# A two-branch attention kernel: PSUM banks, SBUF overlays and load queues of its first stage rearranged

## The chip, the cores and the metric

The kernel runs on one core of a Trainium2 chip. The metric is the time of one execution on the device, in microseconds (us). A core has five engines with a program each: TensorE (PE), VectorE (DVE), ScalarE (ACT), GpSimd (POOL) and SyncE (SP). They run side by side and wait for one another with semaphores; each executes its own instructions in the order in which they stand in its program. Sixteen DMA engines move data between HBM and SBUF; in this kernel the SyncE and ScalarE queues issue to them.

## The reference

Two attention branches read the same input `x` (2048 tokens x 512), and a gate mixes them per token.

```python
g = sigmoid((x * gate_w).sum(-1))
a = A(x)                       # recurrent memory, 64 segments of 32 tokens, one after the other
b = B(x)                       # 4 quarters of 512 tokens
out = g * a + (1 - g) * b

# A, segment s; mem is 8 tokens, first mem0
h = concat(mem, x[s])          # 40 tokens
q, k, v = h@Wq, h@Wk, h@Wv     # 32 heads of 128
o = softmax(mask(q k^T)) v @ Wo
mem, out_a[s] = o[:8], o[8:]

# B, quarter s; 32 heads of 16; M and z are sums over earlier quarters
p = softmax(q k^T + causal) v
mem_part = phi(q) M / (phi(q) z)
o = sig(beta) * mem_part + (1 - sig(beta)) * p
M += phi(k)^T v ;  z += sum phi(k)      # phi(t) = t + 1 for t > 0, else exp(t)
b = o @ wo
```

The kernel writes phi(t) as min(exp(t), 1) + max(t, 0).

## The kernel before

**Program and queues.** The Python code walks through the work once and appends instructions to a list for each engine (`Prog.op`, `Prog.dma`). Dependencies come from named resources: a reader waits for the last writer, a writer for the last writer and all readers. An instruction that waits stops everything behind it on its engine. GpSimd instructions also depend, each, on the GpSimd instruction ahead of them. A DMA frees what it reads only when it has landed.

**Stage one** (`b_projections`) has 64 pieces, numbered `n`. For each quarter of 512 tokens `pk` projects the keys (`wkB`) and the queries (`wqB`) of branch B in four slices of 128 features; the results are copied out of PSUM to staging tiles `stgk` (by VectorE) and `stgq` (by ScalarE), four of each, and stored to DRAM scratch. `pv` projects the values, copied into `V17`, on VectorE and ScalarE in turn, and stored. `kn` transposes a staged key slice, and `phi` makes its features in `phK`. From quarter 1 on `phi` also makes the query features, through a temporary `etmp` (five of them) into `stgp` (three), which are stored. `mz` adds phi(k)^T v to the memory sums in two long-held PSUM banks, from which `MZ16` is masked and stored. `x_chunk` transposes the next 512 tokens of x into `xT`. `gate_parts` computes the gate at pieces 36 and on.

`phi` has three instructions: the exponential on ScalarE at once, and, put off by one piece, a min with 1 (L622) and a max-and-add (L623), both on VectorE.

GpSimd makes constants. `plan_const` sets the first ones; `late_const`, called at piece 9, makes the mask `mneg` of branch A's loop, by memsets and 64 small selects (L414).

**The loads.** x, the three weights of B and small inputs are issued first, on SyncE. x is held in the space of `Wo_sb` until it is transposed. The loop's weights are in a list, `weights`: Wk, Wq and Wv in four loads of 1 MB each, Wo in four, and B's output weights `woB_sb` in eight small ones. Every fourth piece from piece 6 on takes one entry, the rest follow at the end. The big ones are issued on ScalarE's queue, in program order with its other work. First loads of branch B's attention (`bat.load`) come at pieces 50 to 56.

**The loop** (`plan_a`) starts with `left_units(0)`, projections for the memory rows of the first group, and then runs the 64 segments. Each is a hand-written order of units for TensorE (projections L947, mask and scores L1165 to L1172, the output projection L1000), and branch B's attention is woven into it. The loop's tiles (`in_a`) lie over those of stage one (`in_p`) in SBUF. `v.under` lists for each loop tile the stage-one tiles beneath it, and its first writer waits for their last uses: `QT_sb`, for instance, lies over `stgp`, so it waits until the stores from `stgp` have landed. GpSimd copies the x columns of a segment into `hT` (L1124) and the left queries into `QT_sb` (L1334).

**Banks.** `Banks.take` picks one of eight PSUM banks. It holds banks 0 and 1 back for long use, and while few whole pairs are free it prefers a bank whose neighbour is in use, as the loop needs pairs for its wide scores.

Of the kernel before, what the change touches and what calls it, by code (L numbers as in the profile page):

```python
# [5 lines left out]
ALU = mybir.AluOpType  # L6
AX = mybir.AxisListType
BF16 = mybir.dt.bfloat16
F32 = mybir.dt.float32
# [30 lines left out]
class Banks:  # L40
# [3 lines left out]
    def __init__(self, res):  # L44
        self.free = list(range(len(res)))
        self.res = res

    def take(self, long=False):
        assert self.free, "out of banks"
        f = self.free  # L50
        if long:
            c = [b for b in f if b < 2] or f
        else:
            whole = [b for b in f if b > 1 and b ^ 1 in f]
            c = [b for b in f if b not in whole and b > 1] if len(whole) <= 4 else [b for b in f if b > 1]
            c = c or [b for b in f if b > 1] or f
        b = c[0]
        f.remove(b)
        return b
# [165 lines left out]
def build(nc, es, A_x, A_mem0, A_Wq, A_Wk, A_Wv, A_Wo, B_wq, B_wk, B_wv, B_wo, B_beta, gate_w, out, dbg=None):  # L225
    v = NS()
    _, S, DM = A_x.shape
# [29 lines left out]
    def alloc(stack, *specs):  # L257
        at, spans = 0, {}
        for name, shape, dt, n in specs:
# [20 lines left out]
          ("aTg", [128, C, 128], BF16, 0), ("fold", [128, SEG], BF16, 0),  # L280
          ("WH", [128, DM], BF16, 0), ("WL", [128, DM], BF16, 0))
    esP = ExitStack()
    in_p = alloc(esP, ("wkB", [128, C, DM], BF16, 0), ("wqB", [128, C, DM], BF16, 0), ("phK", [128, 4, DM], BF16, 0), ("MZ16", [128, 544], BF16, 0),
          ("bmask", [128, 136], BF16, 0), ("mem0_sb", [128, DM], BF16, 0), ("gwr_sb", [128, 128], BF16, 0), ("beta_sb", [128, HB], BF16, 0),
          ("gB_sb", [128, HB], F32, 0), ("omgB_sb", [128, HB], F32, 0),
          ("etmp", [128, 512], BF16, 5), ("stgp", [128, 512], BF16, 3), ("stgk", [128, 512], BF16, 4), ("stgq", [128, 512], BF16, 4),
          ("V17", [128, 4, HB, 17], BF16, 0), ("wvB", [128, C, DM], BF16, 0))
    esP.close()
    v.stg = {"k": v.stgk, "q": v.stgq, "p": v.stgp}
    v.x_sb = v.Wo_sb[:, 0:NTT, :]  # L290
    esA = ExitStack()
    in_a = alloc(esA, ("xL", [128, C, SEG], BF16, 0), ("LN_sb", [128, 2, 512], BF16, 0), ("KTL", [128, H // 2, SEG, 2], BF16, 2), ("QTL", [128, H // 2, SEG, 2], BF16, 2),
          ("VL", [128, 2, 512], BF16, 2), ("KN_sb", [128, 2, 512], BF16, 0), ("QN_sb", [128, 2, 512], BF16, 0),
          ("KT_sb", [128, H // 2, SEG, 2], BF16, 0), ("QT_sb", [128, H // 2, L, 2], BF16, 0), ("V_sb", [128, 2, 512], BF16, 0),
          ("P_sb", [128, 2, 224], BF16, 0), ("R_sb", [128, 2, 160], F32, 0),
          ("OT_sb", [128, H, L], BF16, 0), ("OTL", [128, H, SEG], BF16, 2),
          ("oTt", [128, 16, 32], F32, 0), ("t1_sb", [128, DM], F32, 0), ("aT_st", [128, C, 128], BF16, 2))
    esA.close()
    v.under = {a: [p for p, (p0, p1) in in_p.items() if p0 < a1 + 64 and a0 < p1 + 64] for a, (a0, a1) in in_a.items()}

# [63 lines left out]
    weights = plan_loads(v, A_x, A_mem0, A_Wq, A_Wk, A_Wv, B_wq, B_wk, B_wv, B_wo, B_beta, gate_w)  # L364
    pieces = b_projections(v)
    bat = v.bat = BAttn(v)
    gates = gate_parts(v)
    x_chunk(v, 0)
    for n in range(len(pieces)):
        if n in (8, 20, 32):  # L370
            x_chunk(v, (n + 4) // 12)
        if n == 9:
            sigmoid(v, v.beta_sb[:, :], v.gB_sb, v.omgB_sb, "gB", [Rs("beta")])
            for src, dst, res in ((v.gB_sb, v.gBp, "gB"), (v.omgB_sb, v.omgBp, "omgB")):
                for j in range(4):
                    q = slice(32 * j, 32 * j + 32)
                    P.op("gp", lambda g, src=src, dst=dst, q=q, j=j: g.tensor_copy(dst[q, :], src[q, :].rearrange("p (f j) -> p f j", j=4)[:, :, j]),
                         reads=[Rs(res)], writes=[Rs(res + "p")], name="%sp%d" % (res, j))
            v.late_const()
        if n >= 36 and n % 2 == 0 and gates:  # L380
            gates.pop(0)()
        pieces[n]()
        if n in (50, 52, 54, 56):
            bat.load(0, n // 2 % 2, "kv"[n // 54])
        if weights and n % 4 == 2 and n > 5:
            weights.pop(0)()
    while weights:
        weights.pop(0)()


    v.home = late_home
    plan_a(v, NSEG_RUN)
    for go in v.g_out:
        if go.count:
# [72 lines left out]
def plan_loads(v, A_x, A_mem0, A_Wq, A_Wk, A_Wv, B_wq, B_wk, B_wv, B_wo, B_beta, gate_w):  # L467
    P, Rs, C, M = v.P, v.Rs, v.C, v.M
    xsrc = A_x[0].rearrange("(i p) d -> p i d", p=128)

    def ld(grp, dst, src, res, name):
        P.dma(P.group(grp), lambda s: s.dma_start(dst, src), writes=[Rs(res)], name=name)

    def x(k):
        for h in range(2):
            o = 4 * k + 2 * h
            ld("x%d%d" % (k, h), v.x_sb[:, o:o + 2, :], xsrc[:, o:o + 2, :], "x_sb%d%d" % (k, h), "dma_x%d%d" % (k, h))
    x(0)
    for nm, dst, src in (("wk", v.wkB, B_wk), ("wq", v.wqB, B_wq), ("wv", v.wvB, B_wv)):
        ld("b" + nm, dst[:, :, :], src.rearrange("(c p) n -> p c n", p=128), nm + "B", "dma_" + nm)  # L480
    x(1)
    g = P.group("small")
    for fn, res in ((lambda s: s.dma_start(v.beta_sb[:, :], B_beta.rearrange("(o n) -> o n", o=1).to_broadcast([128, v.HB])), "beta"),
                    (lambda s: s.dma_start(v.gwr_sb[0:C, :], gate_w.rearrange("(c p) -> c p", p=128)), "gwr"),
                    (lambda s: s.dma_start(v.mem0_sb[0:M, :], A_mem0[0]), "mem0")):
        P.dma(g, fn, writes=[Rs(res)], name="dma_" + res)
    x(2)
    x(3)

    def weight(grp, dst, src, res, c):  # L490
        P.dma(grp, lambda s: s.dma_start(dst[:, c, :], src[c * 128:(c + 1) * 128].rearrange("p h e -> p (h e)")),
              writes=[Rs(res)], name="dma_%s%d" % (res, c), eng="act")
    pend = []
    for res, dst, src in (("Wk", v.Wk_sb, A_Wk), ("Wq", v.Wq_sb, A_Wq), ("Wv", v.Wv_sb, A_Wv)):
        grp = P.group(res)
        for c in range(C):
            pend.append(lambda grp=grp, dst=dst, src=src, res=res, c=c: weight(grp, dst, src, res, c))
    grp = P.group("Wo")
    wosrc = v.A_Wo.rearrange("h e d -> e h d")
    for q in range(4):  # L500
        def wo(q=q):
            P.dma(grp, lambda s: s.dma_start(v.Wo_sb[:, 8 * q:8 * q + 8, :], wosrc[:, 8 * q:8 * q + 8, :]), 
                  writes=[Rs("Wo")] + ([Rs("x_sb%d%d" % (k, h)) for k in (2 * q, 2 * q + 1) for h in range(2)] if q < 2 else []), name="dma_Wo%d" % q, eng="act")
        pend.append(wo)

    def wob():
        grp = P.group("bwo")
        rows = B_wo.rearrange("(f g j d) n -> g j d f n", f=C, g=2, j=4)
        for j in range(4):
            for g in range(2):  # L510
                o = 32 * j + 16 * g
                P.dma(grp, lambda s, j=j, g=g, o=o: s.dma_start(v.woB_sb[o:o + 16, :, :], rows[g, j]), writes=[Rs("woB")], name="dma_woB%d%d" % (j, g))
    pend.append(wob)
    return pend


# [80 lines left out]
def b_projections(v):  # L597
# [14 lines left out]
    def phi(src, rsrc, dst, wres, name, eng, then):  # L612

        n = st["n"] = st["n"] + 1
        et = v.etmp[n % 5][:, :]
        re = Rs("etmp%d" % (n % 5))
        P.op("act", lambda a: a.activation(et, src, ACT.Exp), reads=[rsrc], writes=[re], name=name + "_e")
        if len(dst.shape) == 3:
            src, et = (t.rearrange("p (a d) -> p a d", d=128) for t in (src, et))

        def rest():
            P.op(eng, lambda d: d.tensor_scalar(et, et, 1.0, None, op0=ALU.min), reads=[re], writes=[re], name=name + "_m")  # L622
            P.op(eng, lambda d: d.scalar_tensor_tensor(dst, src, 0.0, et, ALU.max, ALU.add), reads=[rsrc, re], writes=wres, name=name)  # L623
            then()
        later.append(rest)
# [25 lines left out]
    def pv(sb, tt):  # L651
# [7 lines left out]
            return ins  # L659
        P.op("pe", fp, reads=x_res(v, sb) + [Rs("wvB")], writes=[v.rbank[bk]], name="pvn%d_%d" % (sb, tt))  # L660
        rv = Rs("V17_%d" % tt)
        v.evac("act" if tt % 2 else "dve", v.V17[:, tt, :, 0:16], v.pb[bk].rearrange("p (h d) -> p h d", d=16), [bk], [rv], "evv%d_%d" % (sb, tt))
        store("stv%d" % sb, v.vd[sb, :, tt, :], v.V17[:, tt, :, :].rearrange("p h w -> p (h w)"), [rv, Rs("V17o")], [Rs("vd%d_%d" % (sb, tt))],
              "stv%d_%d" % (sb, tt))
        BK.give(bk)
# [248 lines left out]
def plan_a(v, nseg):  # L914
# [208 lines left out]
    def x_copy(s):  # L1123
        P.op("gp", lambda gq: gq.tensor_copy(hT[s % 2][:, :, M:SEG], xT[:, :, SEG * s:SEG * (s + 1) - M]),  # L1124
             reads=x_all, writes=[Rs("hTx%d" % (s % 2))], name="hx%d" % s)

    def segment(s, fill):
# [207 lines left out]
             reads=[Rs("QTL%d_%d" % (par, b)) for b in range(2)], writes=[Rs("QTl")], name="qtl%d" % s)  # L1335
        if s + 1 < nseg:
            x_copy(s + 1)
        for u in ORDER[r]:
            units[u]()

# [88 lines left out]
```

The softmax here doesn't subtract the row's maximum and nothing guards it: scores larger than these inputs give would overflow.

## Time and profile before

| | before |
|---|---|
| time, median of 3 runs | 948.48 us (947.42 to 949.68) |
| span of the profiled run | 946.2 us |
| PE busy | 875.4 us, 93% of the span |
| DVE busy | 635.1 us, 67% |
| ACT busy | 575.4 us, 61% |
| POOL busy | 243.6 us, 26% |
| DMA moved | 51.36 MB, most of it in the first 88 us |
| stage one, first to last projection | from 7.3 to 70.8 us |
| the loop's first segment, to the start of the second | 77.03 to 99.86 us |
| the second segment, to the start of the third | 99.86 to 113.24 us |

Busy time is counted over the whole execution; a stretch of the timeline is needed to see what one stage waits for. In the timeline a row has the start, the length of a run of like instructions, engine, line, output and inputs, the count, and in square brackets the idle time ahead of it with the instruction that ended it. In the bracket a wait that has several causes is put down to the last one.

### The profile page before, as it was taken

How to read it: one execution, taken by the hardware profiler on the slowest of the kernel's cores; microseconds unless marked ns; L12 is line 12 of the kernel's file. 1: busy time of each engine (PE TensorE's matmuls, PEld its weight loads, DVE VectorE, ACT ScalarE, POOL GpSimd, SP SyncE). 2: the span in 40 equal slices, each digit the busy share in tenths (PEclk: the TensorE clock that was granted, in tenths of full speed). 3: DMA queues.
4: the chain of work that ended last, by engine and by line, in shares of the span. 5: the costliest groups of instructions: out<-in, count | busy, mean ns of one | idle time of the engine just before them, and what ended most of it. 6: DMA issues, size and time to landing. Idle time of an engine off the chain costs nothing. (4 is left out here: it accounts for less than half of the span.)

```text
span 946.2 us, 51712 instructions
## 1 busy us (share of the span) xinstructions
PE 875.4 (93%) x23175; PEld 466.7 (49%) x23182; DVE 635.1 (67%) x1388; ACT 575.4 (61%) x1339; POOL 243.6 (26%) x553
## 2 busy tenths in 40 slices
PE   8886989999899999999999989999999999999885
PEld 3443545555454545555455545545455555544442
DVE  4763666676666786776776777667767677677564
ACT  3542666666666766666666665666666666664553
POOL 3610222222222231322222232222222232221110
PEclk9997999999999999999999999999999999999999
DMA  9997000000001121101001110100101110000110
GB/s 305 371 343 247 13 13 16 15 21 18 22 9 38 32 54 28 27 16 27 16 21 49 32 44 20 28 15 19 41 16 41 31 43 24 24 3 9 37 37 8
DMA packets 66052, 51.36 MB, mean 54 GB/s; under 512 B 34464, under 2 KB 64296, under 8 KB 64296
## 3 DMA queue, kind: packets, MB, share of 16 engines
q1 hardware_dynamic: 59944, 31.29, 12.1%
q10 hardware_dynamic: 5888, 16.78, 5.0%
q8 instruction: 182, 2.98, 1.3%
q14 instruction: 38, 0.31, 0.1%
HBM read 33.47 MB, written 14.57 MB: 51 GB/s over the span
## 5 line engine op out<-in xcount | busy, mean ns | idle before, releaser
L801 ACT ACTIVATE PT<-ps 128x1024 bf16<-128x1024 f32 x160 | 163.8, 1024 | 1.8
L947 PE MATMUL ps<-Wv_sb,hT 128*32 128x512 bf16 x2048 | 143.5, 385 | 0.0
L947 PE MATMUL ps<-Wq_sb,hT 128*32 128x512 bf16 x2048 | 134.5, 380 | 0.0
L947 PE MATMUL ps<-Wk_sb,hT 128*32 128x512 bf16 x2048 | 132.7, 379 | 0.0
L808 POOL TENSOR_SCALAR_AFFINE_SELECT PT<-PT 128x512 bf16<-128x512 bf16 (+1 forms) x96 | 75.8, 789 | 199.9 <-ACT PT L801 175.3
L1000 PE MATMUL ps<-Wo_sb,OT_sb 128*32 128x512 bf16 x2048 | 123.4, 380 | 0.3 <-DVE OT_sb L357 0.2
L357 DVE CAST V_sb<-ps 128x512 bf16<-128x512 f32 x128 | 88.5, 691 | 47.7 <-PE ps L947 47.7
L1218 POOL TENSOR_TENSOR P_sb<-P_sb,R_sb 128x64 bf16<-128x64 bf16 x128 | 47.4, 371 | 280.0 <-PE ps L1172 166.7
L959 DVE STREAM_TRANSPOSE QT_sb<-QN_sb 128x256 f32<-128x256 f32 x128 | 56.7, 443 | 77.9 <-ACT QN_sb L355 70.1
L355 ACT ACTIVATE QN_sb<-ps 128x512 bf16<-128x512 f32 x128 | 77.1, 602 | 31.3 <-PE ps L947 28.8
L355 ACT ACTIVATE OT_sb<-ps 128x320 bf16<-128x320 f32 x128 | 56.0, 437 | 61.9 <-PE ps L1241 59.7
L1011 DVE TENSOR_TENSOR WL<-ps,WH 128x256 bf16<-128x256 f32 x128 | 54.3, 424 | 46.0 <-ACT WH L355 42.5
L1181 ACT ACTIVATE P_sb<-ps 128x224 bf16<-128x224 f32 x128 | 45.2, 353 | 60.8 <-PE ps L1172 60.8
L947 PEld LDWEIGHTS ps<-Wk_sb,hT 128*32 128x32 bf16 x2048 | 54.0, 97 | 48.7 <-ACT KN_sb L355 1.2
L357 DVE CAST OT_sb<-ps 128x320 bf16<-128x320 f32 x128 | 61.8, 483 | 20.3 <-PE ps L1241 18.9
L947 PEld LDWEIGHTS ps<-Wq_sb,hT 128*32 128x32 bf16 x2048 | 49.7, 96 | 44.6 <-ACT hT L355 9.3
L959 DVE STREAM_TRANSPOSE KT_sb<-KN_sb 128x256 f32<-128x256 f32 x128 | 56.5, 441 | 21.3 <-ACT KN_sb L355 19.1
L1000 PEld LDWEIGHTS ps<-Wo_sb,OT_sb 128*32 128x32 bf16 x2048 | 48.1, 96 | 45.1 <-DVE OT_sb L357 5.5
L787 PE MATMUL ps<-QTj,KTj 32*128 32x256 bf16 (+1 forms) x768 | 62.9, 255 | 4.3 <-ACT PT L801 3.6
L355 ACT ACTIVATE WH<-ps 128x256 bf16<-128x256 f32 x64 | 24.6, 384 | 62.6 <-PE ps L1000 59.7
L1205 ACT ACTIVATE R_sb<-ps 128x160 f32<-128x160 f32 x128 | 39.1, 305 | 35.8 <-PE ps L1198 35.8
L1228 PE MATMUL ps<-P_sb,V_sb 32*128 32x40 bf16 x2048 | 36.3, 178 | 22.2 <-ACT OT_sb L355 7.7
(131 smaller groups left out, 1578.5 us busy)
## 6 DMA issues: line engine op xcount, KB each, us to landing
Wk_sb<-in_A_Wk_dram ACTq DMA_DIRECT2D x4, 1024.0 KB, 6.9
Wq_sb<-in_A_Wq_dram ACTq DMA_DIRECT2D x4, 1024.0 KB, 8.2
Wv_sb<-in_A_Wv_dram ACTq DMA_DIRECT2D x4, 1024.0 KB, 7.8
Wo_sb<-in_A_Wo_dram ACTq DMA_DIRECT2D x4, 1024.0 KB, 10.9
scr_vd<-V SPq DMA_DIRECT2D x16, 136.0 KB, 6.3
Vj<-scr_vd SPq DMA_DIRECT2D x32, 68.0 KB, 2.5
Wo_sb<-in_A_x_dram SPq DMA_DIRECT2D x8, 256.0 KB, 6.1
scr_kTd<-stgk SPq DMA_DIRECT2D x16, 128.0 KB, 8.0
```

Source lines behind the costliest of these rows:

```text
L355: P.op("act", lambda a: a.activation(dst, src, ACT.Copy), reads=[v.rbank[k] for k in bks], writes=dres, name=name)
L357: P.op("dve", lambda d: d.tensor_copy(dst, src), reads=[v.rbank[k] for k in bks], writes=dres, name=name)
L787: ins = pe.matmul(v.pb[bks[x]][:, 256 * e + o:256 * e + o + w], KT[e][r, 128 * kc:128 * (kc + 1)], QT[r, q0:q0 + w], start=True, stop=True ...
L801: P.op("act", lambda a: a.activation(pt[:, :, :], v.ps[:, bks[0]:bks[1] + 1, :], ACT.Exp, scale=v.SCALE_B), reads=[v.rbank[b] for b in bks ...
L808: P.op("gp", lambda g: g.affine_select(mv, mv, [[0, mv.shape[1]], [1, 128]], ALU.is_ge, 0.0, base=0, channel_multiplier=-1), reads=[rp], w ...
L947: ins = pe.matmul(pb[bk][SEG * j:SEG * (j + 1), :], lhs(c), cols(w, j) if split else w[:, 512 * j:512 * (j + 1)], start=(c == 0), stop=(c ...
L959: P.op("dve", lambda d: d.transpose(to, src), reads=reads, writes=writes, name=name)
L1000: ins = pe.matmul(pb[bk][SEG * j:SEG * (j + 1), :], lhs(4 * k + j), Wo_sb[:, 4 * k + j, :], start=(first and k == ks[0]), stop=False, skip ...
L1011: P.op("dve", lambda d: d.tensor_tensor(lo[:, c], pb[bk][:, c], hi[:, c], ALU.subtract), reads=[rbank[bk], Rs(res[0][hf])], writes=[Rs(res ...
L1181: P.op("act", lambda a: a.activation(P_sb[:, b, :], pb[bk][:, 0:224], ACT.Exp, scale=SCALE), reads=[rbank[bk]], writes=[Rs("P%d" % b), Rs( ...
L1205: P.op("act", lambda a: a.activation(R_sb[:, b, :], pb[bk][:, 224:384], ACT.Ln), reads=[rbank[bk]], writes=[Rs("R%d" % b)], name="ln%d_%d" ...
L1218: P.op(ENG["n"], lambda d: d.tensor_tensor(left(P_sb), left(P_sb), grp04(R_sb[:, b, :]), ALU.mult), reads=[Rs("R%d" % b)], writes=[Rs("P%d ...
```

## The change

Its purpose is to let stage one and the loads beside it run with fewer waits, and to let the loop start without waiting for stores. It has these parts:

- In stage one `Banks.take` gives the bank that came free longest ago (`oldest`); at the start of the loop the old rule returns and the free list is sorted.
- The order of the stage-one tiles and of the loop's tiles is changed, so that the tiles that the first segment writes lie over inputs and temporaries rather than over tiles that are read by stores. `KTL`, `QTL` and `VL`, two of each, are split, and their second ones put last.
- The loads of Wk, Wq and Wv start at piece 2 instead of 6. Wo is taken out of the list and issued on SyncE after all of stage one; `woB_sb` is loaded in segment 1 of the loop.
- The first loads of branch B's attention come at pieces 36 to 42 instead of 50 to 56.
- The min of the query features (L622 before) moves from VectorE to GpSimd; that of the key features stays on VectorE.
- All copies of the values to `V17` are on ScalarE.

```diff
+        self.oldest = True
...
+        elif self.oldest:
+            c = [b for b in f if b > 1] or f
...
-    in_p = alloc(esP, ("wkB", [128, C, DM], BF16, 0), ("wqB", [128, C, DM], BF16, 0), ("phK", [128, 4, DM], BF16, 0), ("MZ16", [128, 544], BF16, 0),
+    in_p = alloc(esP, ("wkB", [128, C, DM], BF16, 0), ("wqB", [128, C, DM], BF16, 0), ("phK", [128, 4, DM], BF16, 0), ("etmp", [128, 512], BF16, 5),
...
-          ("etmp", [128, 512], BF16, 5), ("stgp", [128, 512], BF16, 3), ("stgk", [128, 512], BF16, 4), ("stgq", [128, 512], BF16, 4),
-          ("V17", [128, 4, HB, 17], BF16, 0), ("wvB", [128, C, DM], BF16, 0))
+          ("gB_sb", [128, HB], F32, 0), ("omgB_sb", [128, HB], F32, 0), ("wvB", [128, C, DM], BF16, 0), ("MZ16", [128, 544], BF16, 0),
+          ("stgk", [128, 512], BF16, 4), ("stgq", [128, 512], BF16, 4), ("V17", [128, 4, HB, 17], BF16, 0), ("stgp", [128, 512], BF16, 3))
...
+          ("OT_sb", [128, H, L], BF16, 0), ("OTL", [128, H, SEG], BF16, 2), ("KTL1", LT, BF16, 0), ("QTL1", LT, BF16, 0), ("VL1", [128, 2, 512], BF16, 0),
...
-        if n in (50, 52, 54, 56):
-            bat.load(0, n // 2 % 2, "kv"[n // 54])
-        if weights and n % 4 == 2 and n > 5:
+        if n in (36, 38, 40, 42):
+            bat.load(0, n // 2 % 2, "kv"[n // 40])
+        if weights and n % 4 == 2:
             weights.pop(0)()
-    while weights:
-        weights.pop(0)()
+    v.wo_load()
...
+    v.BK.oldest = False
+    v.BK.free = sorted(v.BK.free)
     plan_a(v, NSEG_RUN)
...
-            P.op(eng, lambda d: d.tensor_scalar(et, et, 1.0, None, op0=ALU.min), reads=[re], writes=[re], name=name + "_m")
+            P.op("gp" if name[3] == "q" else "dve", lambda d: d.tensor_scalar(et, et, 1.0, None, op0=ALU.min), reads=[re], writes=[re], name=name + "_m")
...
-        v.evac("act" if tt % 2 else "dve", v.V17[:, tt, :, 0:16], v.pb[bk].rearrange("p (h d) -> p h d", d=16), [bk], [rv], "evv%d_%d" % (sb, tt))
+        v.evac("act", v.V17[:, tt, :, 0:16], v.pb[bk].rearrange("p (h d) -> p h d", d=16), [bk], [rv], "evv%d_%d" % (sb, tt))
...
+        if s == 1:
+            v.wob_load()
```

More of the change, by code (lines that the diff above doesn't have):

```diff
@@ L282, in build @@
     esP = ExitStack()
-    in_p = alloc(esP, ("wkB", [128, C, DM], BF16, 0), ("wqB", [128, C, DM], BF16, 0), ("phK", [128, 4, DM], BF16, 0), ("MZ16", [128, 544], BF16, 0),
+    in_p = alloc(esP, ("wkB", [128, C, DM], BF16, 0), ("wqB", [128, C, DM], BF16, 0), ("phK", [128, 4, DM], BF16, 0), ("etmp", [128, 512], BF16, 5),
           ("bmask", [128, 136], BF16, 0), ("mem0_sb", [128, DM], BF16, 0), ("gwr_sb", [128, 128], BF16, 0), ("beta_sb", [128, HB], BF16, 0),
-          ("gB_sb", [128, HB], F32, 0), ("omgB_sb", [128, HB], F32, 0),
-          ("etmp", [128, 512], BF16, 5), ("stgp", [128, 512], BF16, 3), ("stgk", [128, 512], BF16, 4), ("stgq", [128, 512], BF16, 4),
-          ("V17", [128, 4, HB, 17], BF16, 0), ("wvB", [128, C, DM], BF16, 0))
+          ("gB_sb", [128, HB], F32, 0), ("omgB_sb", [128, HB], F32, 0), ("wvB", [128, C, DM], BF16, 0), ("MZ16", [128, 544], BF16, 0),
+          ("stgk", [128, 512], BF16, 4), ("stgq", [128, 512], BF16, 4), ("V17", [128, 4, HB, 17], BF16, 0), ("stgp", [128, 512], BF16, 3))
     esP.close()
@@ L291, in build @@
     esA = ExitStack()
[L292 to L296, printed above, removed]
+    LT = [128, H // 2, SEG, 2]
+    in_a = alloc(esA, ("xL", [128, C, SEG], BF16, 0), ("LN_sb", [128, 2, 512], BF16, 0), ("KTL0", LT, BF16, 0), ("QTL0", LT, BF16, 0), ("VL0", [128, 2, 512], BF16, 0),
+          ("KN_sb", [128, 2, 512], BF16, 0), ("QN_sb", [128, 2, 512], BF16, 0), ("KT_sb", LT, BF16, 0), ("QT_sb", [128, H // 2, L, 2], BF16, 0),
+          ("V_sb", [128, 2, 512], BF16, 0), ("P_sb", [128, 2, 224], BF16, 0), ("R_sb", [128, 2, 160], F32, 0),
+          ("OT_sb", [128, H, L], BF16, 0), ("OTL", [128, H, SEG], BF16, 2), ("KTL1", LT, BF16, 0), ("QTL1", LT, BF16, 0), ("VL1", [128, 2, 512], BF16, 0),
           ("oTt", [128, 16, 32], F32, 0), ("t1_sb", [128, DM], F32, 0), ("aT_st", [128, C, 128], BF16, 2))
+    v.KTL, v.QTL, v.VL = [v.KTL0, v.KTL1], [v.QTL0, v.QTL1], [v.VL0, v.VL1]
     esA.close()
@@ L499, in plan_loads, with wo @@
     wosrc = v.A_Wo.rearrange("h e d -> e h d")
[L500 to L504, printed above, removed]
+    def wo():
+        for q in range(4):
+            P.dma(grp, lambda s, q=q: s.dma_start(v.Wo_sb[:, 8 * q:8 * q + 8, :], wosrc[:, 8 * q:8 * q + 8, :]),
+                  writes=[Rs("Wo")] + ([Rs("x_sb%d%d" % (k, h)) for k in (2 * q, 2 * q + 1) for h in range(2)] if q < 2 else []), name="dma_Wo%d" % q)
+    v.wo_load = wo
     def wob():
@@ L512, in wob @@
                 P.dma(grp, lambda s, j=j, g=g, o=o: s.dma_start(v.woB_sb[o:o + 16, :, :], rows[g, j]), writes=[Rs("woB")], name="dma_woB%d%d" % (j, g))
-    pend.append(wob)
+    v.wob_load = wob
     return pend
```

## The prediction

> **What bounds the kernel now.** I read the page's 40 slices first: PE is at 9 or 8 tenths nearly everywhere, so the loop over segments is bound by TensorE, and only the head shows DMA at 9. The head therefore needs a view of its own, the table of stretches:
>
> ```profile
> PEclk9997999999999999999999999999999999999999
> DMA  9997000000001121101001110100101110000110
> ```
>
> ```profile
> 3.00:12.00 9.00, 7.61 (x45) 3.66 (x44) 2.71 (x6) 2.66 (x5) 2.28 (x6) 1.00 1.02 328
> ```
>
> ```profile
> 26.00:71.00 45.00, 37.11 (x293) 19.83 (x299) 31.74 (x66) 23.28 (x41) 17.43 (x60) 1.00 1.01 358
> ```
>
> ```profile
> 84.00:86.00 2.00, 0.00 (x0) 0.00 (x0) 0.00 (x0) 0.00 (x0) 0.00 (x0) 0.50 1.09 381
> ...
> 92.00:94.00 2.00, 2.00 (x30) 0.89 (x24) 0.94 (x2) 1.09 (x3) 0.84 (x2) 0.52 0.00 0
> 94.00:96.00 2.00, 2.00 (x92) 0.99 (x88) 0.79 (x3) 0.93 (x2) 0.25 (x1) 1.00 0.03 8
> ```
>
> Columns: stretch, length, busy time and count of PE, weight load, VectorE, ScalarE, GpSimd, then PE clock, DMA share, GB/s. DMA is full from 3 to 87 us. Between 82 and 86 us no engine works, and the clock stays at half until 94. The timeline there names the cause:
>
> ```profile
> 79.20 0.62 SPq L610 DMA_DIRECT2D scr_pQd<-stgp  x1
> ...
> 86.65 0.45 DVE L959 STREAM_TRANSPOSE QT_sb<-QN_sb 128x256 f32<-128x256 f32 x1 [7.53 <-DMA scr_pQd<-stgp]
> ...
> 87.52 0.38 PE L1165 MATMUL ps<-mneg,ident 128*32 128x224 bf16 x4 [6.86 <-POOL hT L1124]
> ```
>
> QT_sb lies over stgp, whose store, issued at 79.2, lands only at 86.6. The loop's first segment takes 22.83 us (its first projection at 77.03, the second segment's at 99.86), the second one 13.38 (99.86 to 113.24). So the head loses 9.45 us here: 6.9 of wait, some 2.6 of half clock.
>
> The last view is the one on which my forecast turns, GpSimd alone and VectorE alone:
>
> ```profile
> 19.61 0.85 POOL L436 MEMSET mneg<- 128x896 bf16 x1
> ...
> 22.41 4.91 POOL L414 TENSOR_SCALAR_AFFINE_SELECT mneg<-mneg 32x128 bf16<-32x128 bf16 x12
> ...
> 43.73 7.16 POOL L414 TENSOR_SCALAR_AFFINE_SELECT mneg<-mneg 32x128 bf16<-32x128 bf16 x16
> 51.04 0.27 POOL L1124 COPY hT<-xT 128x96 bf16<-128x96 bf16 x1 [0.16 <-POOL mneg L414]
> ```
>
> ```profile
> 25.69 0.39 DVE L622 TENSOR_SCALAR etmp<-etmp 128x512 bf16<-128x512 bf16 x1
> 26.11 0.73 DVE L623 SCALAR_TENSOR_TENSOR stgp<-stgq,etmp 128x512 bf16<-128x512 bf16 x1
> 26.77 0.68 DVE L357 CAST stgk<-ps 128x512 bf16<-128x512 f32 x1
> ```
>
> GpSimd makes the mask mneg without a pause from 19.6 to 50.9 us. VectorE does the first min of the query features at 25.69 and uses it at 26.11.
>
> **The skill.** "GPSIMD Engine Reference", section "Engine selection", calls one-input elementwise work on GpSimd roughly line-rate, and "Elementwise — side-by-side cycle accounting" gives 512 elements in about 0.77 us as its good loop. The trace of before has no such min there; its nearest row, the 128x512 select, takes 0.64. "TensorE: Matmul & The Clock Gate", section "What's actually happening", says that an idle window of about 3.4 us halves the clock and a busy one restores it; the trace agrees roughly: half clock after 3 us idle, full again 6.6 us after work resumed at 87.5. "DMA: Bandwidth & Descriptors", section "Issuing engines are not separate DMA queues", says that loads from ScalarE and SyncE share the 16 engines; the trace agrees, the share being 1.0 whichever queue issues.
>
> **The change, part by part.**
>
> 1. *Min of the query features to GpSimd.* Not in the description, but in the diff: twelve 0.29 us instructions leave VectorE. Their consumer, the 0.7 us max-and-add, stays on VectorE and now waits for GpSimd. GpSimd runs in program order, and the mask's instructions are put into its queue at piece 9, while the first of these mins comes from piece 17. The order of instructions of the changed kernel shows all twelve mins after the last mneg select. So the first cannot start before about 50.9. It takes 0.64 (0.29 as on VectorE to 0.77 by the skill are the ends). With the gap, the waiting VectorE instruction starts at 51.6; I take 51.3, as the mask chain may be a little quicker beside an idle VectorE (64 selects, median 0.25 us with 0.15 between them, so mostly fixed cost).
>  Behind it on VectorE stand the cast of the next key tile, both copies of x chunk 2, and all after. TensorE can run on to the transposes of that key tile (29.90 before), ScalarE to the exponential of them, and six of twelve loop weights are issued by then. Then all stop for some 22 us. No other work fills it: DMA runs dry as the other six loads stand behind ScalarE's wait.
>
> 2. *From the release on.* VectorE does the max-and-add and the cast (0.73 + 0.69): TensorE goes on at 52.7. It starts at half clock: two transposes and three projections of 0.87, doubled, some 6.0 us; then four projections, a transpose and the x transposes, 4 x 0.87 + 0.2 + 1.06, 4.9 us with gaps. So the first projection of quarter 2 (39.72 before) comes at 51.3 + 1.4 + 6.0 + 4.9 = 63.6.
>  Quarter 2 took 18.5 (39.72 to 58.20), quarter 3 12.6 (to 70.80). Their TensorE work alone: 12 projections of 0.87 each, plus products (1.1), transposes, and in quarter 2 the gate dots (4 x 0.54): 15.4 and 11.4.
>
> 3. *Banks in the order they came free* takes away waits for evacuations, and *V casts to ScalarE* takes 8 x 0.69 = 5.5 us off VectorE and adds 8 x 0.60 to ScalarE, which has room (23.3 busy of 45). With the mins (3.5) gone too, quarters 2 and 3 move towards their floors. But six weight loads of 1.05 MB and nearly three quarters' stores (each 12 of 0.131 and 5 of 0.139 MB, 2.3 in all) still have to move, 13 MB, 36 us at 358 GB/s, so store waits remain. I take 17.0 and 12.2: stage one ends at 63.6 + 29.2 = 92.8.
>
> 4. *Weights earlier by one place, output weights on SyncE last, the first K and V loads earlier.* Bytes are the same; the SyncE queue is freer at the end. Output weights are 4.19 MB, issued behind the last store, near 92.8 + 2.3. At 328 GB/s, as one queue gave from 3 to 12 us, 12.8 us; 1.8 to land (the row of the 16 KB KTj loads) and 0.4 of store backlog: they land at 110.1.
>
> 5. *Tiles over inputs, not stores.* The 6.9 us wait goes, and with it the half clock: loop head at 92.8 + 5.7 (6.23 before with a wait of 0.86) = 98.5, first segment 13.38, so the second segment's first projection would be at 111.9. The output projection, 9.3 us into a segment (99.86 to 109.16), would start at 107.8 and waits for the weights to 110.1: +2.3, so 114.2 against 99.86 before, 14.3 us later.
>
> 6. *Other branch's output weights in segment 1*: eight issues on SyncE while DMA is nearly empty, first needed by the tail of the first group, and TensorE's work hides them. *Sorted banks at the loop* rename banks: apart from the first segments, the loop's instructions wait for the same ones as before. Cost nothing.
>
> Sum: 948.5 + 14.3 = 962.8 us.
>
> **Rivals.**
> *A. The stall, but less of it or caught up more*: mask 1.5 us quicker, quarters at their floors (26.8 for 29.2): 3.9 less, 959; with an early landing of the weights, 957. For it: the freed VectorE. Against: DMA still full after the release.
> *B. Output weights later still*: one queue at 281 GB/s (its worst 2 us stretch) and store waits like before (+1.9); TensorE waits over 3 us and falls to half clock (+2.6): 967 to 970.
> *C. Stage one is DMA-bound anyway, so the stall hides*: 948. For it: DMA share 1.01. Against: the stalled ScalarE and SyncE queues issue nothing, so the lost bandwidth isn't regained.
> *D. Faster*: the mins don't queue behind the mask. Then the 9.45 us come back, less 2.3 for the weights: 941. Against: the program order on GpSimd, and each of its instructions waits for the one ahead.
>
> **How the numbers follow.** My case 0.68, A 0.13, B 0.13, C 0.02, D 0.04. The range 957.5 to 969.5 holds my case (959 to 967 with its unknowns: min 0.29 to 0.77, quarters at floor or as before), much of A and B. Slower is 0.94, same 0.02 (C), faster 0.04 (D).
>
> **What would show it.** VectorE, TensorE, ScalarE idle together from about 28 to 51 us, released by a GpSimd min directly after the last mneg select; DMA low from about 38 to 52; half clock after 52; no wait for a store at QT_sb; a wait of 0 to 4 us at the first output projection for Wo_sb; the loop from there on unchanged. I am wrong if the first min runs amid the mask selects, or if quarters 2 and 3 take much more than 31 us.

## The result, and the profile after

| | before | after |
|---|---|---|
| time, median | 949.08 us (947.42 to 950.77, 4 runs) | 964.45 us (961.39 to 965.66, 4 runs) |
| ratio after/before, 95% interval | | 1.0157 [1.0126, 1.0188] |
| span of the profiled run | 946.2 us | 963.9 us |
| stage one ends (first projection L952 of `left_units`) | 70.80 us | 93.20 us |
| loop head (first query projection of the segment) | 77.03 us | 98.38 us |
| second segment's first projection | 99.86 us | 119.24 us |

The change made the kernel slower, by 15.4 us in the medians. Line numbers of after are about five higher than those of before: the min is L627, the max-and-add L628, the projections L952, the output projection L1005.

The page of after, its 40 slices (24 us each): busy share of TensorE, its clock, and share of DMA. In the second slice TensorE is busy for one tenth, and the clock is low in the second and third.

```profile
PE   8188799999899999999999999999999999999885
PEclk9689899999999999999999999999999999999999
DMA  9478600000000112010101111000101110100110
```

The table of stretches of after resolves them to 5 us. As before: stretch, length, busy time of PE, weight load, VectorE, ScalarE and GpSimd, PE clock, DMA share, GB/s.

```profile
30.00:35.00 5.00, 0.00 (x0) 0.00 (x0) 0.00 (x0) 0.00 (x0) 3.20 (x13) 0.64 0.87 337
35.00:40.00 5.00, 0.00 (x0) 0.00 (x0) 0.00 (x0) 0.00 (x0) 3.22 (x14) 0.50 0.01 5
40.00:45.00 5.00, 0.00 (x0) 0.00 (x0) 0.00 (x0) 0.00 (x0) 3.22 (x14) 0.50 0.00 0
45.00:50.00 5.00, 0.00 (x0) 0.00 (x0) 0.00 (x0) 0.00 (x0) 3.68 (x10) 0.50 0.00 0
50.00:55.00 5.00, 3.48 (x12) 1.57 (x13) 4.76 (x10) 1.70 (x3) 2.05 (x2) 0.50 0.31 105
```

For 20 us only GpSimd works, and for 15 of them next to nothing moves on DMA (5 GB/s and less). What it works on is in the timeline of GpSimd in after, and who waits for that in the timeline of VectorE and then of TensorE.

```profile
42.04 6.37 POOL L418 TENSOR_SCALAR_AFFINE_SELECT mneg<-mneg 32x128 bf16<-32x128 bf16 x16
48.58 1.49 POOL L627 TENSOR_SCALAR etmp<-etmp 128x512 bf16<-128x512 bf16 x1 [0.17 <-POOL mneg L418]
```

```profile
50.17 0.69 DVE L628 SCALAR_TENSOR_TENSOR stgp<-stgq,etmp 128x512 bf16<-128x512 bf16 x1 [26.08 <-POOL etmp L627]
...
78.50 0.69 DVE L628 SCALAR_TENSOR_TENSOR stgp<-stgq,etmp 128x512 bf16<-128x512 bf16 x1 [5.32 <-ACT etmp L622]
```

```profile
51.52 0.61 PE L679 MATMUL ps<-ident,stgk 128*128 128x128 bf16 x4 [24.55 <-DVE stgk L360]
...
81.48 0.41 PE L697 MATMUL ps<-V,phK 128*128 128x136 bf16 x4 [3.60 <-DVE phK L628]
...
93.20 1.91 PE L952 MATMUL ps<-Wk_sb,xL 128*32 128x512 bf16 x32 [1.00 <-ACT V L358]
...
108.47 0.39 PE L952 MATMUL ps<-Wk_sb,xL 128*32 128x512 bf16 x2 [2.59 <-issue]
...
113.86 3.30 PE L1005 MATMUL ps<-Wo_sb,OT_sb 128*32 128x512 bf16 x32 [3.26 <-DMA Wo_sb<-in_A_Wo_dram]
```

The first min starts 0.17 us after the last select of the mask, though its input was ready long before; VectorE has waited 26.08 us for it, TensorE 24.55 us for the `stgk` copy behind it. The last row is the second loss: from 110.60 us on the output projection waits for Wo, and then it runs at half clock, 3.30 us where the same 32 matmuls took 1.91 before. The half clock doesn't come from that wait alone. The table of stretches for TensorE (stretch, length, busy time, clock, DMA share, GB/s) shows that the clock had fallen before the wait began, behind the gap of 2.59 us in the row above:

```profile
109.00:110.00 1.00, 1.00 (x44) 0.95 1.11 348
110.00:110.50 0.50, 0.50 (x36) 0.50 1.18 273
```

The wait then kept TensorE at half clock for longer. The queue of SyncE in after shows why Wo is late:

```profile
93.35 1.43 SPq L615 DMA_DIRECT2D scr_vd<-V  x3
94.82 7.54 SPq L507 DMA_DIRECT2D Wo_sb<-in_A_Wo_dram  x4
```

Wo goes out behind the last store of stage one, and its four issues alone take 7.54 us. In the stretch from 95 to 100 us DMA moves 168 GB/s. Right behind Wo, from 102.41 us on, SyncE issues the eight loads of `woB_sb`, so they move beside it.

The query transposition at the loop's head waits for no store any more, as the timeline of VectorE in after shows:

```profile
100.11 0.45 DVE L964 STREAM_TRANSPOSE QT_sb<-QN_sb 128x256 f32<-128x256 f32 x1 [0.80 <-ACT QN_sb L358]
```

### The profile page after: what moved, and what is told of

The parts are those of the page before. It is cut to its first block, busy times and chain, and to the rows that moved or that the text cites. A ratio compares the mean times of both kernels' runs of the same rounds, so it can differ in the third digit from the quotient of the medians.

```text
span 963.9 us, 51722 instructions
## 1 busy us (share of the span) xinstructions
PE 875.8 (91%) x23175; PEld 467.9 (49%) x23182; DVE 626.6 (65%) x1368; ACT 579.3 (60%) x1347; POOL 260.2 (27%) x565
## 4 chain that ended last, share of the span: by engine, by line
PE 82%; ACT 5%; DVE 5%; DMA 3%; POOL 2%; issue 2%; SPq 0%; POOLq 0%; ACTq 0%; DVEq 0%
PE ps L952 43%; PE ps L1005 14%; PE ps L792 5%; PE ps L1233 3%; PE ps L639 3%; PE ps L1027 2%; ACT PT L806 2%; POOL mneg L418 2%; PE ps L1177 2%; DMA Wo_sb<-in_A_Wo_dram 2%; DVE WL L1016 2%; PE ps L1203 1%; PE ps L839 1%; PE ps L1170 1%; PE ps L1246 1%
## 5 line engine op out<-in xcount | busy, mean ns | idle before, releaser
L952 PE MATMUL ps<-Wv_sb,hT 128*32 128x512 bf16 x2048 | 141.8, 381 | 0.0
L952 PE MATMUL ps<-Wq_sb,hT 128*32 128x512 bf16 x2048 | 134.5, 380 | 0.0
L952 PE MATMUL ps<-Wk_sb,hT 128*32 128x512 bf16 x2048 | 132.8, 379 | 0.0
L1005 PE MATMUL ps<-Wo_sb,OT_sb 128*32 128x512 bf16 x2048 | 125.0, 384 | 3.4 <-DMA Wo_sb<-in_A_Wo_dram 3.3
L952 PEld LDWEIGHTS ps<-Wk_sb,hT 128*32 128x32 bf16 x2048 | 54.2, 97 | 48.5 <-ACT KN_sb L358 1.2
L1186 ACT ACTIVATE P_sb<-ps 128x224 bf16<-128x224 f32 x128 | 45.2, 353 | 53.4 <-PE ps L1177 51.3
L1005 PEld LDWEIGHTS ps<-Wo_sb,OT_sb 128*32 128x32 bf16 x2048 | 48.7, 96 | 49.4 <-DVE OT_sb L360 5.5
L952 PEld LDWEIGHTS ps<-Wq_sb,hT 128*32 128x32 bf16 x2048 | 49.9, 96 | 44.5 <-ACT hT L358 9.3
```

The source lines that it names most:

```text
L952: ins = pe.matmul(pb[bk][SEG * j:SEG * (j + 1), :], lhs(c), cols(w, j) if split else w[:, 512 * j:512 * (j + 1)], start=(c == 0), stop=(c ...
L1005: ins = pe.matmul(pb[bk][SEG * j:SEG * (j + 1), :], lhs(4 * k + j), Wo_sb[:, 4 * k + j, :], start=(first and k == ks[0]), stop=False, skip ...
L1186: P.op("act", lambda a: a.activation(P_sb[:, b, :], pb[bk][:, 0:224], ACT.Exp, scale=SCALE), reads=[rbank[bk]], writes=[Rs("P%d" % b), Rs( ...
```

## The experiments

Two questions: whether the min behind the mask is the whole of the loss, and what the other parts are worth. Each ratio is against the kernel before, timed on the same chip. The runs were spread over several chips, so sizes of effects are taken from the ratios; 0.1% is about 0.95 us.

**The min alone, taken back.** Edit of after:

```diff
-            P.op("gp" if name[3] == "q" else "dve", lambda d: d.tensor_scalar(et, et, 1.0, None, op0=ALU.min), ...)
+            P.op(eng, lambda d: d.tensor_scalar(et, et, 1.0, None, op0=ALU.min), ...)
```

> The changed kernel with one edit: the min of the query features is back on VectorE, all else stays changed. Theory (the min queues behind the mask on GpSimd, and VectorE, TensorE and ScalarE stop behind it): the 24.6 us stop of TensorE at the key transpose is gone, and since the wait for a store at the loop's start is gone too, this is faster than the kernel before: the second segment's first projection at 94 to 96 us instead of 99.9 before and 119.2 changed, so about 944 us (940 to 947). Some wait for the output weights (2 to 5 us) stays. Rival (the slow-down comes from the output weights on SyncE, from the bank order or from the SBUF order, and the stop only moves slack): still 955 us or more.

Measured: 945.05 us (941.84 to 948.88), ratio 0.9973 [0.9959, 0.9986]. The stop is gone; stage one ends at 68.82 us instead of 93.20, and the ratio is 0.0184 below that of after, some 17.5 us. The timeline of TensorE in this kernel shows what takes part of the gain:

```profile
92.29 3.60 PE L1005 MATMUL ps<-Wo_sb,OT_sb 128*32 128x512 bf16 x32 [5.61 <-DMA Wo_sb<-in_A_Wo_dram]
```

With an earlier loop the wait for Wo grows from 3.26 to 5.61 us. So in these two profiles the stop hid some of the second loss. The second segment starts at 98.99 us here, not at 94 to 96 as expected. In this run too the clock fell before the wait: it was 0.71 in the mean from 84 to 85 us and 0.50 from there on, and the wait began at 86.7.

**The min on GpSimd, but not behind the mask.** The first 30 selects and memsets of the mask are put at the start, the others are put into the program one for each piece from piece 3 on:

```diff
+    for _ in range(30):
+        v.mask_todo.pop(0)()
...
-            v.late_const()
...
+        if n > 2 and v.mask_todo:
+            v.mask_todo.pop(0)()
```

> The changed kernel with the min of the query features still on GpSimd, but the mask's instructions not all ahead of it: thirty of them are issued at the very start, where GpSimd idled for 11 us, the rest one after each piece from piece 3 on. Theory (the place in GpSimd's queue is what costs, not the engine): no stop of more than 3 us in VectorE for a min, and a time like that of the kernel with the min back on VectorE, 941 to 949 us. Rival (the min takes 1.49 us on GpSimd against 0.29 us on VectorE, and that slowness itself holds VectorE up, twelve times): some 12 x 1.2 = 14 us slower than with the min back on VectorE, so 955 us or more.

Measured: 944.63 us (940.28 to 948.29), ratio 0.996 [0.9946, 0.9973]. The mins are on GpSimd as in after, each between a few selects. The waits of VectorE in this kernel (total, times, longest):

```profile
DVE stgp L644 <- POOL etmp L643: 8.2, 6, 3.3
```

The same wait was up to 26.1 us in after; the longest here, 3.3 us, is a little over the 3 us expected. GpSimd is thus not too slow for the min: it was the place in its queue.

**The min alone, put into before.**

```diff
-            P.op(eng, lambda d: d.tensor_scalar(et, et, 1.0, None, op0=ALU.min), ...)
+            P.op("gp" if name[3] == "q" else "dve", lambda d: d.tensor_scalar(et, et, 1.0, None, op0=ALU.min), ...)
```

> The kernel before with one edit: the min of the query features moves to GpSimd, nothing else changes. Theory: TensorE stops from about 28 to 51 us here too, and as DMA is less behind afterwards a few us are caught up: 18 to 24 us slower than before, 967 to 973 us; slower than the whole change, which has the other edits to its credit. Rival (the slow-down is made by other parts of the change): 949 us, as before.

Measured: 976.02 us (975.21 to 976.88), ratio 1.0293 [1.0261, 1.0324], above the expected 967 to 973. The waits of TensorE in this kernel:

```profile
PE ps L634 <- DVE etmp L622: 26.0, 1, 26.0
PE ps L1165 <- POOL hT L1124: 6.1, 1, 6.1
```

This one edit makes before slower by some 28 us. The stop of 26.0 us comes, and the old wait at the loop's head stays beside it (6.1 for 6.86 us): nothing of the stop is regained, while in after the other parts give back some 13 us (ratios 1.0293 and 1.0157).

**Half of the stop.** The mask is made right after the first constants instead of at piece 9:

```diff
+    v.late_const()
...
-            v.late_const()
```

> The changed kernel with one edit: the mask is made right after the first constants instead of at piece 9, so GpSimd, which idled from 5.6 to 17 us, starts it some 13 us sooner; it stays wholly ahead of the mins. Theory (the stop lasts until the mask ends): the first min starts near 36 us instead of 48.6, TensorE's stop shrinks from 24.6 to about 12 us, and the time with it, to 952 us (950 to 955), between the changed kernel (964.5) and the one with the min back on VectorE (945). Rival (any stop cools TensorE and upsets the stores, whatever its length): 960 us or more.

Measured: 954.21 us (950.97 to 956.75), ratio 1.0067 [1.0042, 1.0091]. The waits of TensorE:

```profile
PE ps L679 <- DVE stgk L360: 13.7, 1, 13.7
```

The stop is 10.9 us shorter than in after (24.55), the ratio 0.0090 lower, some 8.5 us. The loss follows the length of the queue ahead of the first min.

**Wo back on ScalarE's list**, without the stop (e4) and with it (e6). Edit of both; e4 has the min on VectorE as well:

```diff
-    v.wo_load()
+    while weights:
+        weights.pop(0)()
...
+            P.dma(grp, ..., name="dma_Wo%d" % q, eng="act")
+    for q in range(4):
+        pend.append(lambda q=q: wo(q))
```

> The changed kernel with the min back on VectorE and the four output-weight loads back in the list on ScalarE's queue (pieces 50, 54, 58 and 62), B's output weights still late. Theory (DMA is full in all of stage one, so the bytes end at the same time wherever they are issued, but on SyncE behind the last store the queue runs empty before): no wait for the output weights at the first output projection, stage one's stores slower; 1 to 4 us faster than with the min back alone, 939 to 944 us. Rival (putting them last is what frees the stores): as fast or slower than with the min back alone.

> The changed kernel with one edit: the four output-weight loads are back in the list on ScalarE's queue, the min stays on GpSimd behind the mask. Theory (3.3 us of wait for the output weights and the half clock after it are a loss of its own, which adds to the stop): no wait for Wo_sb at the first output projection; 4 to 8 us faster than the changed kernel, 956 to 960 us. Rival (with the stop, DMA has idled so long that the weights' place no longer matters): 962 to 966 us.

Measured: e4 940.54 us (938.54 to 945.24), ratio 0.9928 [0.9904, 0.9951]; e6 960.7 us (957.28 to 962.42), ratio 1.0119 [1.0088, 1.015], slightly above what was expected. In neither does TensorE wait for Wo. With after and e1 these four make a square:

| | min behind the mask | min on VectorE | difference |
|---|---|---|---|
| Wo last, on SyncE | 1.0157 [1.0126, 1.0188] | 0.9973 [0.9959, 0.9986] | 0.0184, 17.5 us |
| Wo on ScalarE's list | 1.0119 [1.0088, 1.015] | 0.9928 [0.9904, 0.9951] | 0.0191, 18.1 us |
| difference | 0.0038, 3.6 us | 0.0045, 4.3 us | |

The two losses add up: about 18 us for the stop, about 4 for Wo. The second is small against the intervals, which overlap in the left column and just part in the right one; that the wait itself is gone, the traces of e4 and e6 show.

**Smaller parts**, on the way to the best version. e7 is e4 with the first K and V loads back at pieces 50 to 56; e8 is e2 with Wo on ScalarE's list; e11 is e8 with those loads at 50 to 56.

```diff
-        if n in (36, 38, 40, 42):
-            bat.load(0, n // 2 % 2, "kv"[n // 40])
+        if n in (50, 52, 54, 56):
+            bat.load(0, n // 2 % 2, "kv"[n // 54])
```

> The kernel with the min back on VectorE and the output weights on ScalarE's queue (940.5 us), and now also the first K and V loads of branch B back at pieces 50 to 56. Theory: at pieces 36 to 42 these ten small issues take 6 us of SyncE's time in quarter 2 and hold up stores, for which VectorE waited 13.3 us there; at 50 to 56 the wait moves to quarter 3 rather than goes: within 2 us, 939 to 943 us. Rival (the early place is what lets the loop start on time): 3 us slower or more.

> The changed kernel with the mask spread over the pieces (min still on GpSimd, 944.6 us) and the output weights on ScalarE's queue. Theory (the two repairs are independent): as with the min back on VectorE, 3 to 5 us come back, 940 to 942 us. Rival (VectorE's relief of 3.5 us counts once the other waits are gone): below 939 us.

> As e8_spread_wo_act (939.23 us: the minimum on GpSimd with the mask made in pieces, the output weights on ScalarE's list), with the K and V loads at pieces 50 to 56 as before. If the later loads gain nothing: 936 to 939 us, the same as e8 or 1 to 2 us faster, as e7 was against e4. If they keep stores from waiting: 940 to 942 us.

Measured: e7 938.45 us (936.26 to 942.51), ratio 0.9901 [0.987, 0.9933]; e8 939.23 us (938.77 to 939.65), ratio 0.9905 [0.9886, 0.9923]; e11 937.74 us (934.42 to 940.48), ratio 0.9899 [0.9866, 0.9931]. e7 and e8 are a little faster than the main case of what was expected. All three beat both kernels, by 1.0% against before and some 24 us against after; among them nothing can be told apart. So the place of the K and V loads isn't shown to matter, and the min may be on either engine once it doesn't queue behind the mask.

The trace of e7 has one more thing to say of the half clock. TensorE never waits for Wo there, and yet the first output projection runs at half clock, behind a gap of 1.89 us:

```profile
86.89 0.39 PE L953 MATMUL ps<-Wk_sb,xL 128*32 128x512 bf16 x2 [1.89 <-issue]
...
88.79 3.50 PE L1006 MATMUL ps<-Wo_sb,OT_sb 128*32 128x512 bf16 x32
```

e6 has such a gap, of 2.08 us, and no half clock after it (1.91 us for the projection), so the gap doesn't bring it every time.

**Banks and tiles.** e9 is e7 with the old order of the banks in stage one (`self.oldest = False`), e10 is e7 with the old layout of the tiles, e12 has both old.

```diff
-         self.oldest = True
+         self.oldest = False
```

> The minimum on VectorE, the output weights on ScalarE's list and the K and V loads at pieces 50 to 56 (as in e7_best_old_loads, 938.45 us), but the stage-one banks taken in turn as before. If the order of the banks matters, TensorE waits for fixed banks again in stage one (before: 2.5 us for the bank behind the piece, 1.1 us and less for V), which the stage's DMA hides in part: 0 to 4 us slower than e7, 938 to 943 us. If DMA alone bounds stage one: within 1 us of e7. If the order of the banks were the gain of 10 us: about 948 us.

> As e7_best_old_loads (938.45 us), but the loop's tiles laid out as before, so that the first query tiles lie over inputs of stores. If this layout is what took the wait away: VectorE waits at the first query transposition for a store again (6.9 us before), the loop's head is that much later and the clock halves once: 944 to 948 us. If the other transfers hide it: 938 to 940 us.

> As e7_best_old_loads, with both the old order of the banks and the old layout; what is left of the change is V's copies on ScalarE, weights from piece 2 on and the other branch's output weights later. Each old part alone measured 940 to 941 us, 2 us or less above e7. If the two do the same work (stores of stage one no longer hold the loop's head, either because stage one ends earlier or because nothing lies over them), then without both the loop's head waits 5 to 7 us for a store and the time is that of the kernel before, 945 to 949 us. If the gain of e7 is in the parts that are left: 940 to 943 us, as the two alone.

| | new tiles | old tiles |
|---|---|---|
| new banks | e7: 938.45, ratio 0.9901 [0.987, 0.9933] | e10: 939.93, ratio 0.9928 [0.9908, 0.9948] |
| old banks | e9: 941.0, ratio 0.9931 [0.9904, 0.9958] | e12: 944.37, ratio 0.9958 [0.9947, 0.997] |

e10 missed its expectation of 944 to 948: the wait for a store is back, yet little is lost. The timeline of VectorE in e10, and then in e12:

```profile
80.40 0.45 DVE L965 STREAM_TRANSPOSE QT_sb<-QN_sb 128x256 f32<-128x256 f32 x1 [6.00 <-DMA scr_pQd<-stgp]
```

```profile
84.28 0.45 DVE L965 STREAM_TRANSPOSE QT_sb<-QN_sb 128x256 f32<-128x256 f32 x1 [6.26 <-DMA scr_pQd<-stgp]
```

The wait is as long in both, but it ends at 80.40 and 84.28 us (86.65 in before). In e10 the last of these stores is issued at 72.82 us, in e12 at 76.27, in before at 79.20; each lands some 7.5 to 8 us later. With the old tiles, the new order of the banks brings TensorE to the loop's head earlier (72.12 us for 77.10) and the last store out earlier; TensorE then waits for it. In e9 and e7 nothing waits for that store at the loop's head, but TensorE gets there later: it goes on with the scores at 82.24 in e9 and 80.95 in e7, against 81.27 in e10. In these four executions either part alone starts the second segment earlier than e12 (97.06 us) by as much as both do: at 93.53 us in e10, 93.55 in e9 and 94.36 in e7. The times don't show such an overlap: as ratios, the new banks are worth 0.0030 with either layout, and the new layout 0.0027 with either order of the banks. Each of these is within the intervals. Both old cost 0.0057, some 5.4 us, against both new, and that is separated; how it divides is open. e12, which was expected at 945 to 949 or at 940 to 943, came between: it is still 0.42% below before, with V's copies on ScalarE, the earlier weights, the later `woB_sb` and the sorted list of banks at the loop left of the change. Which of these does it wasn't tried.

## Why the prediction was right

The forecast was 962.8 us and 14.3 us slower; measured were 964.45 and 15.4. Several steps were off and offset each other.

1. *The start of the waiting VectorE instruction, 51.3 us.* Measured 50.17. The mechanism is as foretold: a wait in program order, with all of VectorE, TensorE and ScalarE behind it. "PSUM — Partial Sum Buffer" in the Trainium skill, section "Engine vs sequencer instructions", calls the queues of VectorE, ScalarE and GpSimd strict FIFO; e1, e2 and e5 show the price here. Two sizes were off. The mask ended at 48.4, not 50.9: its last 16 selects began 1.7 us earlier than in before, at 42.04, and took 6.37 us, where before they took 7.16 beside a busy VectorE. And the first min took 1.49 us, not 0.64; it lies above both ends of the forecast, 0.29 and the 0.77 from "GPSIMD Engine Reference". The measurement decides.
2. *Quarter 2 at 63.6 us.* Measured 60.97. The clock was at half for a shorter time than the 6.0 us assumed: TensorE worked at half clock from 51.5 to about 55.3.
3. *Quarters 2 and 3 at 17.0 and 12.2 us.* Measured 14.3 (60.97 to 75.27) and 17.9 (75.27 to 93.20), together 3.0 us more than forecast. The floor of 15.4 for quarter 2 was counted too high: the same 148 matmuls between the two marks keep TensorE busy for 14.89 us in before and for 14.19 in after, where it hardly waits. Quarter 3 has the store waits: VectorE stood 5.32 us before 78.50, TensorE 3.60 us before 81.48, and the clock fell to half again. The profile's bracket there names the exponential, but that had long been done; what was missing is a `stgp` tile whose store had not landed. That store, issued at 66.53 us, took 11.9 us to land. The moved K and V loads were issued just behind it, from 67.56 to 73.14, and shared the DMA engines with it. That they held it up isn't shown: VectorE has such waits in e6, with these loads at the same place, and in e7, with them at the old one. The end of stage one, 92.8, was then hit (93.20) by errors of both signs.
4. *Wo landing 15.0 us after its issue at 95.1.* Issued at 94.82, it landed at about 113.8, 19 us later. The rate was the term that was wrong: 328 GB/s was taken from the head of the kernel; here it was 168 from 95 to 100 us, while SyncE needed 7.54 us to issue the four, then some 350 to 360 up to 110, and 120 from 110 to 115. Part 6 of the prediction erred too: it put the loads of `woB_sb` at nothing because DMA would be nearly empty. They were issued while DMA was full with Wo (a share of 1.06 from 100 to 105 us) and landed from 111.6 to 115.1. Their 0.52 MB at 350 GB/s is 1.5 us, an estimate of the most that they took from Wo; no run moved them alone.
5. *The loop head at 98.5 us without a wait for stores.* Measured 98.38, with no such wait. *Second segment at 114.2.* Measured 119.24. The output projection started 3.8 us later than the forecast's 110.1, and lost 1.4 at half clock. The gap of 2.59 us named "issue", which wasn't foreseen, adds nothing to this as long as Wo lands at 113.8: without it TensorE would have waited for Wo by that much longer. But the clock fell behind it. "TensorE: Matmul & The Clock Gate" in the Trainium skill, section "What's actually happening", has the clock fall after an idle window of some 3.4 us, in windows that run free of the kernel; here it had fallen by 110 us, when the longest idle stretch just before was 2.59. The measurement decides: no 3.4 us of unbroken idleness were needed. The long wait and the half clock of rival B thus happened, on top of the main case, but the clock fell before the wait and not by it.
6. *The end.* The second segment starts 19.4 us later than before in the profiled runs, but the span is only 17.7 longer and the median 15.4. From that point to the end the profiled runs take 844.3 to 847.4 us, so those 1.7 us can't be put down to anything here; the other 2.3 are the spread of the runs: the profiled run of after was 1.2 us above its median, that of before 1.1 below. At the second segment the forecast was 5.0 us short. That the total came out within 1.1 us is in part luck.

Rival C, that the stop hides behind DMA, is out: in e3 all of it arrives at the end. Rival D, the change without the stop, was put at 941; e1 measured 945.05, and most of the 4 us between can be put down to Wo, whose wait was 5.61 us there for the 2.3 allowed: e4, without it, measured 940.54. Where the forecast valued the store wait at 9.45 us and gave all of it to the layout, the runs give some 5.4 to banks and layout together, without showing how it divides.

## What to carry to other kernels

Before moving a small operation to an idle-looking engine, look at what is queued ahead of it there at the moment when it is first needed: mean busy time (26% for GpSimd) says nothing of a stretch of 30 us in which constants are made. If one fast engine waits for it in program order, the whole pipeline stops; interleave the long work with the short, as e2 did, and the move is harmless. A load that only the end of a stage is free to issue should be asked when it is first used; a gain from taking one wait away is worth only the distance to the next wait, so try parts together and apart.

## What the runs showed of the hardware

- A min of 128x512 bf16 in place took 1.49 us on GpSimd in after, also when VectorE was idle beside it (1.83 to 2.00 in three of the twelve), and 0.29 us on VectorE: five times as long.
- Four loads of 1 MB, with rows of 1 KB, issued back to back on SyncE took 7.54 us to issue in after, 1.9 us each in the mean; two back to back on ScalarE took 4.01 us in before. Issued singly on ScalarE in e4, the same loads took 0.38 to 0.41 us each. DMA moved 168 GB/s in the first 5 us of the four, and why it started so slowly isn't shown.
- In the loop's first segment TensorE has a gap of 2.59 us in the midst of one group of projections, ended by "issue" alone. e1 (2.31), e2 (2.41), e4 (1.07), e5 (2.24), e6 (2.08), e7 (1.89) and e11 (0.50) have it at the same place; before, e3, e8, e10 and e12 don't, and e9 has one of 1.70 a little later. DMA is full beside it in after (a share of 1.03 to 1.16), but not in e7 (0.44 and 0.07 in the two stretches of 1 us from 85 on). A 16 KB packet of the instruction queue, of 1.14 us, starts with the gap in after; that it is the cause isn't shown.
- The clock of TensorE fell to half 1.4 us after that gap in after, before any longer wait, and 1.8 us after the gap of 1.89 us in e7; in e6 it did not fall after one of 2.08 us.
